# Where the operands of a fused attention, MoE and MLP kernel are split and rounded: VectorE, GpSimd, and which stage

## The chip, the cores and the metric

One Trainium2 chip, one of its cores. The metric is the device time of one execution in microseconds (us). The kernel before takes 1073.9 us, the median of three runs (1072.25 to 1073.95).

## The reference

Three layers, one after the other, in fp32. The outputs of each are the tokens of the next.

```python
# retention-like attention: batch 4, 8 heads, 768 steps, head size 64
state = gamma * state + k[t] (x) v[t];   y[t] = scale * q[t] @ state
# 3072 tokens of 512 -> mixture of 8 experts with a capacity of 384 tokens each:
# all (token, expert) logits in descending order, each token goes to the first expert with room
h = maximum(x[mask] @ w1[e], 0);  out[mask] = h @ w2[e]        # 512 -> 1024 -> 512
# one MLP shared by all tokens
h = x @ w_in;  g = where(h > 0, h, exp(minimum(h, 0)) - 1)     # 512 -> 2048
return g @ w_out                                               # 2048 -> 512
```

`w_in` and `w_out` come as 64-bit words, two per pair of columns, since the kernel rounds them itself ("chunks" below).

## The kernel before, in words

**Three stages.** Attention runs over 48 steps of 64 tokens (4 batches of 12). Then the routing of the first expert (phase 0) is searched with nothing else to do for TensorE. Then eight experts follow one another. Each handles its 384 tokens through both of its own matrices (entries `L1` and `L2` of an order list, 8 each) and then through the shared MLP (entries `F1` and `F2`, 16 each), and scatters its rows to the output. While expert n runs, VectorE searches the routing of later experts, and GpSimd gathers their weights and rows by indirect DMA.

**Products in three parts.** Every matmul operand is split in a high part `hi` (a ScalarE copy to the 32-bit replicated format) and a low part `lo = x - hi` (one subtraction). A product is hi*hi + hi*lo + lo*hi (`mm3`, lines 673 to 676). For the expert matrices `prep` makes `hi` on ScalarE (line 663) and `lo` on GpSimd (line 666), except for the tiles that the table `BYV` gives to VectorE: `L1` number 2 and `L2` number 0 of each expert. For the shared matrices `Wide.parts` makes `hi` (line 274) and `lo` on GpSimd in four pieces of 128 columns (line 279), once per tile. The low part is stored in DRAM and read back for later experts (lines 280 and 270). `which` is 0 for `w_in` and 1 for `w_out`.

**Chunks.** The 32 tiles of `w_in` and `w_out` are loaded as raw words by ScalarE's DMA queue into three staging buffers, and each tile ("chunk") takes three steps: two VectorE instructions (lines 253 and 254), one ScalarE instruction (line 256) and then the load of a later chunk, one GpSimd addition (line 260). During attention `side(j)` is called about twice per step of 64 tokens and starts a step of a chunk on three of eight calls. Ten chunks are done there. In phase 0 of routing the tiles of these ten are split (`early`, before line 806). The other 22 chunks are done during expert 0, at times that `CONV` lists.

**ELU.** For each `F1` tile: Exp on ScalarE from PSUM (line 733), on VectorE min and add, then the max with PSUM, then `gh` on ScalarE (line 740) and `gl = g - gh` on VectorE.

**Order.** The order of instructions on each engine is written out by the program. A model clock advances with the matmuls (`tick`), and `at(us, fn)` puts `fn` in the program when the clock reaches its time. Each engine runs its own queue in that order and waits for what an instruction needs. Router steps are generators; after `yield "v"` the next step is put behind the time `V.free` when the model thinks VectorE is free. `Paced` adds each router, ELU and split instruction to `V.free`. The chunk instructions use `nc.vector` itself, so `V.free` does not count them. VectorE instructions that go through `Paced` have line 215 in the profile.

Of the kernel before, what the change touches and what calls it, by code (L numbers as in the profile page):

```python
# [10 lines left out]
F32 = mybir.dt.float32  # L11
# [13 lines left out]
BIG = 6.0e37  # L25
WARM2 = (2, 2, 2, 2, 14)
WARM3 = (4, 4, 6)
GAP = {"w": 1.8, "x": 1.0, "t": 2.5}
ROOM = {"L1": 2, "L2": 3, "F1": 3, "F2": 3}
BYV = (("L1", 2), ("L2", 0))  # L30
RSTART = 6
PACE, AFTER, HOLD = 0.4, 0.5, 7.0
CONV = {"L1": (0.4, 1.3), "L2": (0.4,), "F1": (0.4, 1.3), "F2": (0.4,)}
ELU = (1.6, 2.6)
NWARM = 18
STAGES, EVERY = 3, 8
SUB = 4
MORE, LOWS = 2, 3
EACH = [(30 - 3 * i, 2 if i == 0 else 3) for i in range(11)]
LEVELS = [(27, 5), (22, 5), (17, 5), (12, 5), (7, 5), (2, 5), (0, 2)]  # L40
# [178 lines left out]
class Wide:  # L219
# [25 lines left out]
        next(self.steps, None)  # L245

    def chunks(self):
        V = self.nc.vector
        for i in range(32):
            t = self.stage.pop(i)  # L250
            lo, hi = t[:, 0:1024:2], t[:, 1:1024:2]
            m = self.raw[i % 2][i // 2].bitcast(I32)
            V.tensor_scalar(m, hi, 3, 0x3FFFFFFF, op0=OP.logical_shift_left, op1=OP.bitwise_and)
            V.scalar_tensor_tensor(m, hi, -0x40000000, m, op0=OP.bitwise_and, op1=OP.bitwise_or)
            yield
            self.nc.scalar.activation(lo, lo.bitcast(U32), AF.Copy, scale=2.0 ** -29)
            if i:
                self.load()
            yield
            self.nc.gpsimd.tensor_tensor(m, m, lo, OP.add)  # L260
            self.done = i + 1
            yield

    def parts(self, which, f, pool, later):


        nc, name = self.nc, ("wis", "wos")[which]
        lo = pool.tile([128, 512], F32R, name=name, bufs=LOWS)
        if (which, f) in self.high:
            nc.sync.dma_start(lo.bitcast(F32), self.low[which, f])  # L270
            return self.high[which, f], lo
        hi = self.high[which, f] = self.pools[which].tile([128, 512], F32R, name="w")
        src = self.raw[which][f]
        nc.scalar.activation(hi, src, AF.Copy)

        def low():
            for c in range(0, 512, 128):
                s = slice(c, c + 128)
                nc.gpsimd.tensor_sub(lo[:, s], src[:, s], hi[:, s].bitcast(F32))  # L279
            nc.sync.dma_start(self.low[which, f], lo.bitcast(F32))  # L280

        later(low)
        return hi, lo


class Router:
# [126 lines left out]
    def search_each(self, ph, Lm, M):  # L413


        nc, w, V = self.nc, self.w, self.V
        vm, vt = w("vm", [128, NCOL, E]), w("vt", [128, 192])
        V.tensor_scalar(vm, M, BIG, -BIG, op0=OP.mult, op1=OP.add)
        V.tensor_tensor(vm, vm, Lm, OP.add)
        yield "v"  # L420
        p = self.pm()
        nc.tensor.transpose(p[:, 0:128], vm[:, 0:16].rearrange("p c e -> p (c e)"), self.ident)
        nc.tensor.transpose(p[0:64, 128:256], vm[:, 16:24].rearrange("p c e -> p (c e)"), self.ident)
        yield "p"
        nc.scalar.activation(vt[:, 0:128], p[:, 0:128], AF.Copy)
        nc.scalar.activation(vt[0:64, 128:192], p[0:64, 128:192], AF.Copy)
        nc.scalar.activation(vt[64:128, 128:192], p[0:64, 192:256], AF.Copy)
        Tb, ni, n = w("Tb", [128, 1], I32), w("ni", [128, 1], I32), w("n", [128, 1])
        cand, pre = w("candf", [128, 8], I32), w("pref", [128, 8], I32)
        cnt, sat = w("cnt", [128, 8], BF), w("satf", [128, 8])  # L430
        scr = [w(f"scr{j}", [128, 192], BF) for j in range(3)]
        yield "a"
        for i, (k, r) in enumerate(EACH):
            J = (1 << r) - 1
            cf = self.jf[:, 0] if i == 0 else cand
            if i > 1:
                V.scalar_tensor_tensor(cand[:, :J], ni.to_broadcast([128, J]), EACH[i - 1][0], pre[:, :J],
                                       op0=OP.logical_shift_left, op1=OP.bitwise_xor)
            for j in range(J):
                V.tensor_scalar(scr[j % 3], vt, cf.bitcast(F32)[:, j:j + 1], 0.0, op0=OP.is_ge, op1=OP.add,  # L440
                                accum_out=cnt[:, j:j + 1])
                if j % SUB == SUB - 1 and j < J - 1:
                    yield "v"
            if i > 1:
                V.scalar_tensor_tensor(Tb, ni, EACH[i - 1][0], Tb, op0=OP.logical_shift_left, op1=OP.bitwise_xor)
            if 0 < i < len(EACH) - 1:
                Jn = (1 << EACH[i + 1][1]) - 1
                V.tensor_tensor(pre[:, :Jn], self.jf[:, i + 1, :Jn], Tb.to_broadcast([128, Jn]), OP.bitwise_xor)
            yield "v"
            p = self.pm()  # L450
            nc.tensor.matmul(p[:, :J], self.same, cnt[:, :J], start=True, stop=True)
            yield "p"
            V.tensor_scalar(sat[:, :J], p[:, :J], self.remp, 0.0, op0=OP.is_ge, op1=OP.add, accum_out=n)
            V.tensor_copy(ni, n)
            if i == 0:
                Jn = (1 << EACH[1][1]) - 1
                self.first_sign(Tb, ni, k)
                V.tensor_tensor(cand[:, :Jn], self.jf[:, 1, :Jn], Tb.to_broadcast([128, Jn]), OP.bitwise_xor)
        V.scalar_tensor_tensor(Tb, ni, 0, Tb, op0=OP.logical_shift_left, op1=OP.bitwise_xor)
        yield "v"  # L460
        p = self.pm()
        nc.tensor.transpose(p[:, :E], Tb.bitcast(F32)[0:E].to_broadcast([E, 128]), self.ident[0:E, 0:E])
        yield "p"
        T = w("T", [128, 1])
        V.tensor_reduce(T, p[:, :E], AX.X, OP.max)
        self.T = T
# [122 lines left out]
def mlps(nc, tc, ctx, a, xd, out, router, wide, ident, acc, rot, pms):  # L589
# [39 lines left out]
    def at(us, fn):  # L629
        heapq.heappush(heap, (clock[0] + us, next(serial), fn))  # L630
# [9 lines left out]
    def run_router():  # L640
        if clock[0] < hold[0]:
            return at(hold[0] - clock[0], run_router)
        after = next(phases[0], None)
        if after is None:
            phases.pop(0)
        if phases:
            at(max(PACE, V.free - clock[0] + PACE) if after == "v" else AFTER, run_router)

    def start_phase(ph):
        phases.append(router.phase(ph))  # L650
# [3 lines left out]
    def prep(ck):  # L654
        kind, n, f = ck
        if kind in ("F1", "F2"):
            WSP[ck] = wide.parts(kind == "F2", f, sb, lambda low: at(0.6, low))
            return
        which = "w1" if kind == "L1" else "w2"
        src = WS[n, which, f // 2][:, (f % 2) * 512:(f % 2) * 512 + 512]  # L660
        hi = sb.tile([128, 512], F32R, name=which + "h", bufs=ROOM[kind])
        lo = sb.tile([128, 512], F32R, name=which + "l", bufs=ROOM[kind])
        nc.scalar.activation(hi, src, AF.Copy)  # L663

        def low():
            (V if (kind, f) in BYV else nc.gpsimd).tensor_sub(lo, src, hi.bitcast(F32))  # L666
            if f in (1, 3):
                gather_w(n, which, f // 2 + 2)

        at(0.6, low)  # L670
        WSP[ck] = (hi, lo)
# [57 lines left out]
    def elu(n, f, p):  # L729
        g = sb.tile([128, CAP], F32, name="g")  # L730
        gh = sb.tile([128, CAP], F32R, name="gh", bufs=4)
        gl = sb.tile([128, CAP], F32R, name="gl", bufs=4)
        nc.scalar.activation(g, p, AF.Exp)  # L733

        def lower():
            V.tensor_scalar(g, g, 1.0, -1.0, op0=OP.min, op1=OP.add)
            V.tensor_tensor(g, p, g, OP.max)

        at(0.5, lower)
        at(ELU[0], lambda: nc.scalar.activation(gh, g, AF.Copy))  # L740
        at(ELU[1], lambda: V.tensor_sub(gl, g, gh.bitcast(F32)))
        GS[n, f] = (gh, gl)

    def do_F2(n, f):
# [57 lines left out]
        return acc.tile([128, 512], F32, name="acc")[:, :384]  # L802

    router.spare = spare
    early = iter(range(wide.done))
    for _ in router.phase(0):
        tick(1.0)
        i = next(early, None)
        if i is not None:
            wide.parts(i % 2, i // 2, sb, lambda low: low())  # L810
        if 0 in router.es and (0, "w1", 0) not in WS:
            gather_w(0, "w1", 0)
            gather_w(0, "w2", 0)
        if 0 in router.idx and (0, 0) not in XG:
            for tb in range(3):
                gather_x(0, tb)
            advance(1)
# [29 lines left out]
    for i, ck in enumerate(seq):  # L847
# [5 lines left out]
            run_todo(n + 1)  # L853
        advance(i + LA)
        if n == 0:
            for us in CONV[kind]:
                at(us, wide.step)
        do[kind](n, f)
    tick(10.0)

# [2 lines left out]
def body(ctx, tc, a, xd, out):  # L863
# [26 lines left out]
        return pms.tile([128, 512], F32, name="pm")  # L890

    router = Router(nc, st, wk, pm, a, L, ident)

    attention(nc, tc, a, xd, ident, side, router.columns)
    acc = ctx.enter_context(tc.tile_pool(name="acc", bufs=4, space=PSUM))
# [93 lines left out]
```

## Time and profile before

| | |
|---|---|
| time, median of 3 runs | 1073.9 us (1072.25 to 1073.95) |
| the profiled execution: its own time, its span | 1078.4 us, 1076.6 us |
| granted TensorE clock, mean | 0.964 |
| busy: TensorE, its weight loads, VectorE, ScalarE, GpSimd | 92%, 83%, 68%, 33%, 39% |
| HBM | 143.75 MB read, 20.97 MB written |

The span runs from the first to the last instruction. The rest of the execution's own time lies around it. A matmul record covers its whole passage through the array, and matmuls follow one another more closely than they last, so the distance of their starts is what counts.

### The profile page before, as it was taken

To read this page: it belongs to the slowest core of one execution; us is meant where nothing else is said; L and a number is where in the kernel's file an instruction comes from. 1 tells how busy PE (TensorE), PEld (TensorE's weight loads), DVE (VectorE), ACT (ScalarE), POOL (GpSimd) and SP (SyncE) were. 2 spreads that over 40 slices of the span, in tenths; PEclk is the share of its full clock that TensorE was granted. 3 is DMA by queue.
4 is the path that set the end of the run, shared out by engine and by line. 5 is a ranking of instruction groups with operands and counts; after the bars stand their busy time and mean duration, and the time that the engine had idled before them with its cause. 6 is when DMAs were issued, how large, how long until landed. Compare 5 with 4: busy or idle time off the path is not lost.

```text
span 1076.6 us, 20354 instructions
## 1 busy us (share of the span) xinstructions
PE 992.8 (92%) x7730; PEld 891.6 (83%) x7730; DVE 732.7 (68%) x2294; ACT 350.5 (33%) x712; POOL 424.3 (39%) x508
## 2 busy tenths in 40 slices
PE   8888938798789999999999999999999999999995
PEld 6777825786678988898899889988998898999994
DVE  4664677879999777977897789778977514331431
ACT  3443422233344323332333233223322333233221
POOL 5465575637898021702170217021702181026001
PEclk9998957899899999999999999999999999999998
DMA  9798535446534263327422742373237326432441
GB/s 367 239 344 289 186 131 189 136 138 194 192 119 161 80 225 120 106 83 228 127 91 89 225 127 89 97 226 118 89 98 226 117 91 212 120 110 84 132 123 49
DMA packets 69635, 166.06 MB, mean 154 GB/s; under 512 B 8992, under 2 KB 15776, under 8 KB 69536
## 3 DMA queue, kind: packets, MB, share of 16 engines
q1 hardware_dynamic: 51152, 101.67, 28.9%
q0 software_dynamic: 13056, 46.14, 13.0%
q10 hardware_dynamic: 5328, 16.94, 4.7%
q8 instruction: 61, 1.00, 0.4%
q14 instruction: 38, 0.31, 0.1%
HBM read 143.75 MB, written 20.97 MB: 153 GB/s over the span
## 4 chain that ended last, share of the span: by engine, by line
PE 71%; DVE 19%; issue 3%; POOL 3%; DMA 2%; ACT 1%; another core or an unknown queue 0%; POOLq 0%; SPq 0%; DVEq 0%; ACTq 0%
PE pr L674 10%; PE pr L676 10%; PE pr L675 10%; PE acc L752 8%; PE acc L753 7%; PE acc L754 7%; DVE scr L215 3%; PE acc L674 3%; PE acc L675 3%; PE acc L676 3%; PE py L138 2%; DVE Tb L215 2%; PE pq L107 2%; DVE g L215 2%; DVE candf L215 2%
## 5 line engine op out<-in xcount | busy, mean ns | idle before, releaser
L674 PE MATMUL pr<-yh,w 128*128 128x384 f32 x512 | 178.0, 348 | 1.3 <-DVE g L215 1.3
L676 PE MATMUL pr<-yh,wis 128*128 128x384 f32 x512 | 174.1, 340 | 0.0
L675 PE MATMUL pr<-yl,w 128*128 128x384 f32 x512 | 172.5, 337 | 0.0
L666 POOL TENSOR_TENSOR w1l<-sw,w1h 128x512 fp32r<-128x512 f32 x56 | 73.0, 1305 | 249.5 <-ACT w1h L663 229.6
L752 PE MATMUL acc<-w,gh 128*128 128x512 f32 x384 | 156.4, 407 | 0.0
L754 PE MATMUL acc<-w,gl 128*128 128x512 f32 x384 | 152.4, 397 | 0.8 <-DVE gl L215 0.8
L753 PE MATMUL acc<-wos,gh 128*128 128x512 f32 x384 | 153.1, 399 | 0.0
L600 POOL DMA_INDIRECT sw<-in_w,es x64 | 66.4, 1038 | 165.0 <-DVE es L215 142.0
L215 DVE TENSOR_SCALAR_CACHE_REDUCE scr<-vt,candf 128x192 bf16<-128x192 f32 x350 | 124.3, 409 | 1.8
L733 ACT ACTIVATE g<-pr 128x384 f32<-128x384 f32 x128 | 62.8, 491 | 183.5 <-PE pr L676 171.8
L740 ACT ACTIVATE gh<-g 128x384 fp32r<-128x384 f32 x128 | 67.1, 525 | 169.5 <-DVE g L215 167.5
L215 DVE TENSOR_SCALAR g<-g 128x384 f32<-128x384 f32 x128 | 52.6, 411 | 84.8 <-ACT g L733 84.0
L674 PEld LDWEIGHTS pr<-yh,w 128*128 128x128 f32 x512 | 97.3, 190 | 7.5 <-DVE g L215 2.0
L675 PEld LDWEIGHTS pr<-yl,w 128*128 128x128 f32 x512 | 97.1, 190 | 4.0
L676 PEld LDWEIGHTS pr<-yh,wis 128*128 128x128 f32 x512 | 96.7, 189 | 0.2 <-POOL wis L279 0.2
L676 PE MATMUL pr<-xh,w1l 128*128 128x384 f32 x256 | 88.4, 345 | 4.1 <-POOL w1l L666 3.9
L215 DVE TENSOR_TENSOR gl<-g,gh 128x384 fp32r<-128x384 f32 x128 | 74.0, 578 | 25.6 <-ACT gh L740 24.4
L674 PE MATMUL pr<-xh,w1h 128*128 128x384 f32 x256 | 89.3, 349 | 1.8 <-ACT w1h L663 1.8
L754 PEld LDWEIGHTS acc<-w,gl 128*128 128x128 f32 x384 | 73.0, 190 | 18.6 <-DVE gl L215 1.2
L674 PE MATMUL acc<-hh,w2h 128*128 128x384 f32 x256 | 87.8, 343 | 0.0
L675 PE MATMUL pr<-xl,w1h 128*128 128x384 f32 x256 | 87.3, 341 | 0.3 <-DVE xl L215 0.3
L676 PE MATMUL acc<-hh,w2l 128*128 128x384 f32 x256 | 85.9, 336 | 0.0
(187 smaller groups left out, 2091.2 us busy)
## 6 DMA issues: line engine op xcount, KB each, us to landing
wis<-low SPq DMA_DIRECT2D x117, 256.0 KB, 3.1
wos<-low SPq DMA_DIRECT2D x117, 256.0 KB, 2.7
Q<-in_kq SPq DMA_DIRECT2D x15, 768.0 KB, 8.0
V<-in_kv SPq DMA_DIRECT2D x15, 768.0 KB, 8.3
stg<-in_w_in ACTq DMA_DIRECT2D x16, 512.0 KB, 4.8
stg<-in_w_out ACTq DMA_DIRECT2D x16, 512.0 KB, 4.2
x_rows<-xs SPq DMA_DIRECT2D x32, 192.0 KB, 7.6
low<-wis SPq DMA_DIRECT2D x16, 256.0 KB, 2.0
```

Source lines behind the costliest of these rows:

```text
L107: nc.tensor.matmul(p[lo, pr, :], q[hi, 1, pr], q[hi, 0, pr], start=True, stop=True)
L215: return getattr(self.eng, name)(*args, **kw)
L600: nc.gpsimd.indirect_dma_start(out=t, out_offset=None, in_=a[f"{which}_{pair}"], in_offset=bass.IndirectOffsetOnAxis(ap=router.es[n][:, :1 ...
L666: (V if (kind, f) in BYV else nc.gpsimd).tensor_sub(lo, src, hi.bitcast(F32))
L674: nc.tensor.matmul(p, ah, bh, start=first, stop=False)
L675: nc.tensor.matmul(p, ah, bl, start=False, stop=False)
L676: nc.tensor.matmul(p, al, bh, start=False, stop=last)
L733: nc.scalar.activation(g, p, AF.Exp)
L740: at(ELU[0], lambda: nc.scalar.activation(gh, g, AF.Copy))
L752: nc.tensor.matmul(p, gh[:, s], wh, start=f == 0, stop=False)
L753: nc.tensor.matmul(p, gh[:, s], wl, start=False, stop=False)
L754: nc.tensor.matmul(p, gl[:, s], wh, start=False, stop=f == 15)
```

## The change

The low parts of the first expert matrix (`L1`) all go to VectorE, those of `L2` all to GpSimd. The low parts of `w_in` go to VectorE, those of `w_out` to GpSimd, in one instruction of 512 columns instead of four of 128. ELU becomes two ScalarE passes (Relu of -h, then Exp of minus that, which is exp(min(h, 0))) and one VectorE step, `max(g - 1, h)`, with later times in the model clock. `side` starts chunk steps on three of every four calls, the split of finished chunks in phase 0 is gone, and chunk instructions go through `Paced`. In expert 0 a chunk step is put in only when the model thinks VectorE free within 1 us, or when the tile is needed within four entries. The pause in the middle of a counting level of the router (`"s"`) is shorter, that after a ScalarE copy (`"a"`) longer.

```diff
-GAP = {"w": 1.8, "x": 1.0, "t": 2.5}
+GAP = {"w": 1.8, "x": 1.0, "t": 1.5}
-BYV = (("L1", 2), ("L2", 0))
-ELU = (1.6, 2.6)
+ELU = (2.0, 2.8, 3.8)
-STAGES, EVERY = 3, 8
-SUB = 4
+STAGES, EVERY = 3, 4
+SUB, AHEAD = 4, 4
     def chunks(self):
-        V = self.nc.vector
+        V = self.V
         def low():
-            for c in range(0, 512, 128):
-                s = slice(c, c + 128)
-                nc.gpsimd.tensor_sub(lo[:, s], src[:, s], hi[:, s].bitcast(F32))
+            (nc.gpsimd if which else self.V).tensor_sub(lo, src, hi.bitcast(F32))
                 if j % SUB == SUB - 1 and j < J - 1:
-                    yield "v"
+                    yield "s"
         if phases:
-            at(max(PACE, V.free - clock[0] + PACE) if after == "v" else AFTER, run_router)
+            wait = V.free - clock[0]
+            at({"v": max(0.0, wait) + PACE, "s": max(0.1, wait - 0.1), "a": 2.0}.get(after, AFTER), run_router)
         def low():
-            (V if (kind, f) in BYV else nc.gpsimd).tensor_sub(lo, src, hi.bitcast(F32))
+            (V if kind == "L1" else nc.gpsimd).tensor_sub(lo, src, hi.bitcast(F32))
-        nc.scalar.activation(g, p, AF.Exp)
-
-        def lower():
-            V.tensor_scalar(g, g, 1.0, -1.0, op0=OP.min, op1=OP.add)
-            V.tensor_tensor(g, p, g, OP.max)
-
-        at(0.5, lower)
-        at(ELU[0], lambda: nc.scalar.activation(gh, g, AF.Copy))
-        at(ELU[1], lambda: V.tensor_sub(gl, g, gh.bitcast(F32)))
+        nc.scalar.activation(g, p, AF.Relu, scale=-1.0)
+        nc.scalar.activation(g, g, AF.Exp, scale=-1.0)
+        at(ELU[0], lambda: V.scalar_tensor_tensor(g, g, -1.0, p, op0=OP.add, op1=OP.max))
+        at(ELU[1], lambda: nc.scalar.activation(gh, g, AF.Copy))
+        at(ELU[2], lambda: V.tensor_sub(gl, g, gh.bitcast(F32)))
-    early = iter(range(wide.done))
     for _ in router.phase(0):
         tick(1.0)
-        i = next(early, None)
-        if i is not None:
-            wide.parts(i % 2, i // 2, sb, lambda low: low())
         if n == 0:
+            late = 2 * (f + AHEAD) if kind in ("F1", "F2") else 0
             for us in CONV[kind]:
-                at(us, wide.step)
+                at(us, lambda: (wide.done < late or V.free < clock[0] + 1.0) and wide.step())
     router = Router(nc, st, wk, pm, a, L, ident)
+    wide.V = router.V
```

## Rows read from the trace of the kernel before

**Rows 1.** Busy time by stage: PE, PEld, DVE, ACT, POOL; clock, DMA share, GB/s.
```profile
0.00:136.00 136.00, 116.80 (x2724) 102.33 (x2726) 77.45 (x195) 53.50 (x124) 72.49 (x110) 0.95 0.80 282
...
176.00:228.00 52.00, 44.47 (x317) 40.66 (x318) 39.34 (x68) 16.78 (x33) 30.44 (x25) 0.90 0.42 141
228.00:320.00 92.00, 76.18 (x415) 65.19 (x414) 85.99 (x195) 37.43 (x75) 68.95 (x102) 0.93 0.53 175
...
427.00:534.00 107.00, 106.00 (x586) 96.13 (x585) 86.37 (x328) 33.90 (x70) 32.85 (x32) 1.00 0.43 134
```

**Rows 2.** Timeline of PE in expert 1: start, duration, line, form.
```profile
400.74 0.34 PE L674 MATMUL pr<-yh,w 128*128 128x384 f32 x1
...
402.84 0.40 PE L752 MATMUL acc<-w,gh 128*128 128x512 f32 x1
...
404.25 0.60 PE L622 MATMUL px<-ident,row 128*128 128x128 f32 x4
```

**Rows 3.** VectorE groups, 176 to 320 us: busy, mean ns, idle before.
```profile
L254 DVE SCALAR_TENSOR_TENSOR w<-stg,w 128x512 int32<-128x512 int32 x22 | 18.2, 829 | 0.8
L253 DVE TENSOR_SCALAR w<-stg 128x512 int32<-128x512 int32 x22 | 18.1, 824 | 0.0
L215 DVE TENSOR_SCALAR g<-g 128x384 f32<-128x384 f32 x15 | 12.1, 805 | 0.5 <-ACT g L733 0.5
L215 DVE TENSOR_TENSOR cmp<-v,cand 128x372 bf16<-128x372 f32 (+1 forms) x12 | 11.6, 1007 | 0.2
...
L215 DVE SCALAR_TENSOR_TENSOR hl<-pr,hh 128x384 fp32r<-128x384 f32 x8 | 4.4, 552 | 1.5 <-ACT hh L688 1.5
```

**Rows 4.** Timeline of VectorE while GpSimd had no tensor work.
```profile
208.43 1.01 DVE L215 TENSOR_TENSOR cmp<-v,cand 128x372 bf16<-128x372 f32 x2
...
209.65 0.42 DVE L253 TENSOR_SCALAR w<-stg 128x512 int32<-128x512 int32 x1
210.10 0.69 DVE L254 SCALAR_TENSOR_TENSOR w<-stg,w 128x512 int32<-128x512 int32 x1
```

**Rows 5.** VectorE's removed ELU pass, 427 to 534 us.
```profile
L215 DVE TENSOR_SCALAR g<-g 128x384 f32<-128x384 f32 x16 | 5.7, 357 | 4.6 <-ACT g L733 4.4
```

**Rows 6.** Timeline in expert 0, 189 to 195 us: VectorE, GpSimd, PE.
```profile
189.09 5.10 DVE L215 TENSOR_TENSOR cmp<-v,cand 128x372 bf16<-128x372 f32 x2
...
192.51 1.27 POOL L666 TENSOR_TENSOR w2l<-sw,w2h 128x512 fp32r<-128x512 f32 x1
...
194.25 0.48 PE L399 MATMUL pm<-cmp,M 128*8 128x31 bf16 x12 [3.03 <-DVE cmp L215]
```

**Rows 7.** Groups of the whole span: busy, mean ns, idle before.
```profile
L215 DVE TENSOR_SCALAR_CACHE_REDUCE scr<-vt,candf 128x192 bf16<-128x192 f32 x350 | 124.3, 409 | 1.8
...
L666 POOL TENSOR_TENSOR w1l<-sw,w1h 128x512 fp32r<-128x512 f32 x56 | 73.0, 1305 | 249.5 <-ACT w1h L663 229.6 <-DVE hl L215 11.5 <-DVE sat L215 5.0
...
L740 ACT ACTIVATE gh<-g 128x384 fp32r<-128x384 f32 x128 | 67.1, 525 | 169.5 <-DVE g L215 167.5 <-issue 2.0
...
L279 POOL TENSOR_TENSOR wos<-w 128x128 fp32r<-128x128 f32 x64 | 33.0, 546 | 5.1 <-ACT w L274 3.0 <-issue 2.0
...
L215 DVE TENSOR_TENSOR w1l<-sw,w1h 128x512 fp32r<-128x512 f32 x8 | 5.5, 686 | 3.6 <-ACT w1h L663 3.6
```

**Rows 8.** Waits of SyncE's DMA queue in attention: total us, times, longest.
```profile
SPq L71 <- DMA stg<-in_w_out: 19.6, 3, 7.8
```

**Rows 9.** Chain that ended last, 25 to 60 us: shares by line.
```profile
by line: DMA V<-in_kv 47.3%; issue 11.9%; PE py L138 8.8%; PE pq L107 8.2%; PE pS L128 7.4%; PE pT L156 4.5%; POOL V L115 4.2%; PE pL L171 3.6%; PE pS L127 3.2%; PE pq L108 1.2%; SPq L71 0.2%; POOLq L115 0.1%
```

**Rows 10.** Timeline of routing phase 0, one of five equal levels.
```profile
144.23 1.45 DVE L215 TENSOR_TENSOR cmp<-v,cand 128x372 bf16<-128x372 f32 x2
```

**Rows 11.** Timeline of GpSimd and ScalarE at the start of expert 0.
```profile
171.54 2.50 POOL L666 TENSOR_TENSOR w1l<-sw,w1h 128x512 fp32r<-128x512 f32 x2
...
182.50 0.63 ACT L663 ACTIVATE w1h<-sw 128x512 fp32r<-128x512 f32 x1 [3.55 <-DMA sw<-in_w,es]
```

**Rows 12.** Waits of PE, 345 to 1060 us: total, times, longest.
```profile
PE pr L676 <- POOL w1l L666: 3.4, 6, 0.7
```

## The prediction

> **What bounds the kernel now.** I read the stages first, then inside each the engine that is waited for. In the table by stage [rows 1] an expert in steady state, 427 to 534 us, has TensorE busy for 106.00 of 107 us at full clock, so little is left there. The timeline of one such expert [rows 2] gives the need: an `F1` tile takes 402.84 - 400.74 = 2.10 us for its 12 matmuls, and six of 512 columns take 1.41 us, 0.235 each. Eight `L1`, eight `L2` and sixteen `F1` tiles at 2.10 us and 144 matmuls at 0.235 us make 101 us; the rest to 107 is transposes, router products and about one us of waiting.
>
> Expert 0 is another matter. Its matmuls run from 176 to 320 us, which is 144 us for the work of 107, and the clock is at 0.90 and 0.93. VectorE is busy for 39.34 + 85.99 = 125.3 us of it [rows 1]. That busy time isn't all work. The groups of this stretch [rows 3] beside the same forms elsewhere [rows 4, 5] show: the chunk's first instruction takes 0.824 against 0.42, its second 0.829 against 0.69, the ELU pass 0.805 against 0.357, a comparison of the router 1.007 against half of 1.01. Over 22, 22, 15 and 12 instructions that is 8.9 + 3.1 + 6.7 + 6.0 = 24.7 us in which VectorE stood inside an instruction. The timeline shows on what [rows 6]: a pair of comparisons begun at 189.09 ends at 194.2, just after the last of an unbroken row of GpSimd tensor instructions (192.51 + 1.27 = 193.8), and TensorE, whose next product needs the comparison, stands 3.03 us. The step `hl`, which has one operand in PSUM and one in SBUF, isn't stretched: 0.552 in this crowded stretch [rows 3]. [...]
>
> **The change, part by part.**
>
> *Attention.* The condition on `sides` is met at 8 to 10, 12 to 14, up to 92 to 94 of 95 calls: 22 chunks, where 10 were done (the title's 24 is not what I count). Twelve more chunks cost VectorE 12 x (0.42 + 0.69) = 13.3 us and GpSimd about 12 x 1.3 = 16 us, in idle time of 136 - 77.45 = 58.5 and 63.5 us [rows 1, 4, 7]. The loads are the doubtful part: 12 x 0.524 = 6.3 MB. The DMA share is 0.80 at 282 GB/s, 352 GB/s when busy; 6.3 MB take 17.9 us, and 0.20 x 136 = 27 us are idle. So the lower bound is 0. For the upper bound: SyncE's loads of keys and values already wait for landings of chunks, 19.6 us in three waits for one of the matrices [rows 8], and in the stretch where this happens 47.3% of 35 us, 16.6 us, of the chain that ended last is a late load of `V` [rows 9]. With 12 more loads beside 10 that grows by 12/10 x 16.6 = 20 us. I take +9, the middle, since the last third of the extra loads falls behind the last load of keys and values.
>
> *Phase 0.* The ten early splits leave. A pair of comparisons beside them took 1.45 us [rows 10] against 1.01 [rows 4], 0.44 on each of five levels, 2.2 us on the only chain that TensorE has there; the small instructions of each level are stretched as well, unknown, bounded by as much again. -2 to -5, I take -3.5.
>
> *Start of expert 0.* Two low parts of 2.50 us stand on GpSimd ahead of the gather of the second weights, and ScalarE then waits 3.55 us for that landing [rows 11]. They move to VectorE (2 x 0.686 [rows 7], ahead of router steps that nobody awaits). I take -2, bounds 0 and -2.5.
>
> *Expert 0.* VectorE: 125.3 - 24.7 = 100.6 us without the stretching. Twelve chunks leave, -13.3; the ELU pass leaves, 16 x 0.357 = -5.7; the new single step costs what `hl` costs, 0.552, against 0.558 for the old max, so nothing; sixteen `w_in` parts arrive, 16 x 0.686 = +11.0; six more `L1` parts, +4.1. That makes 96.7 us. GpSimd: 99.4 us of busy time [rows 1] lose 12 chunks (16), 11 `w_in` tiles at 4 x 0.546 (24), seven `L1` parts (9.1), gain one `L2` part, while sixteen `w_out` tiles at 1.3 cost what eleven at 4 x 0.546 cost less 3: about 49 us, half. With half of GpSimd's work I halve the stretching, 12.3 us: VectorE 109 us. That is about TensorE's own 107. If VectorE keeps the 18.7 us that it is idle now (144 - 125.3), expert 0 takes 128 us, -16; if TensorE sets it alone, 108, -36. I take 120, -24: VectorE's order is now planned with the chunks counted, so router products are placed when their inputs are done, but `w_in` and `w_out` parts are still cut at the same moments by the two engines. ScalarE's added ELU pass (16 x 0.525 [rows 7]) and ten more `hi` copies, less twelve chunk steps, fit in its idle 90 us [rows 1].
>
> *Experts 1 to 7.* The wait for the `L1` low part on GpSimd goes: -3.4 us [rows 12], up to -6 with the weight loads that start late behind it. Against it stands the ELU chain at the first `F1` tiles. There tile 2 needs tile 0's PSUM, one tile (2.10 us) later; two ScalarE passes (taken as the 0.525 of `gh` [rows 7] each) and the step (0.552) take 1.6, which fits by half a us if VectorE is free. `gh` of tile 0 now stands behind the two passes of tile 1, which cannot start before 2.10, so it ends at 2.10 + 3 x 0.525 = 3.7 and `gl` at about 4.2 us, and `F2` wants it at 2 x 2.10 + 2 x 0.235 = 4.67. Four counting steps of the router, each up to 0.409 [rows 7], in front of it would cost 1.2 us, at most 8 us in seven experts. I take +1: together -3, bounds -6 and +5. `L1` parts on VectorE add 6 x 0.686 = 4.1 us an expert and the removed pass takes 5.7: VectorE stays below TensorE. `GAP` and the router's pauses change only the order of work with slack: 0.
>
> Sum: +9 - 3.5 - 2 - 24 - 3 = -23.5. The profiled execution takes 1078.4 us, 4.5 above the median, so 1054.9 for it and 1050 for the median.
>
> **The rivals.**
>
> *Attention eats more* (0.15). The loads cost the full 20 us: -12.5, 1061. For it: the late `V` load [rows 9]. Against: an idle DMA share of 0.20.
>
> *The relief is complete* (0.17). The loads hide (0 to +2) and TensorE alone sets expert 0 (-36): about -42, 1032. For it: 96.7 us of VectorE work below 107. Against: stretching doesn't vanish.
>
> *Slower: chunk loads pace attention* (0.11). VectorE runs in order, and a chunk's first instruction now stands seven `side` calls behind its load instead of fifteen. Two steps of 64 tokens last 136/24 = 5.7 us, so seven calls are about 10 us; a queue wait of up to 7.8 [rows 8] and the transfer could exceed that, and then VectorE, and with it attention, stands once for each chunk. Over 22 chunks it decides from 33/22 = 1.5 us a chunk, where it eats the 32.5 of the other terms; at 3 us a chunk the time is 1073.9 + 66 - 32.5 = 1107, at 2 us 1085.
>
> *The moved parts are held* (0.05). A subtraction with two SBUF inputs may wait for a GpSimd instruction of 1.3 us each time. In expert 0 that is 22 moved parts x 1.3 = 29 us of VectorE, 126 us instead of 97, as busy as before; then expert 0 gains only about 8 and the time is 1066. Against: the eight such parts in the trace average 0.686 with no sign of it [rows 7]. [...]
>
> **How the numbers follow.** The forecast has 0.52, its own range 1038 to 1061. Below 1030 and above 1074 I leave about 0.09 each: 1030 to 1074 reaches to the complete relief and the costlier attention and holds the held parts. Slower by more than 0.2% (what a measurement of this kernel can tell from none) is 0.11 for the slower rival and 0.01 from the edges, within 0.2% 0.05 from the upper edges of the cases that gain and the lower edge of the one that loses, faster the remaining 0.83.
>
> **What would show it.** Attention longer than 136 us, with more waits of SyncE's queue for chunks; phase 0 shorter by some 3 us with comparisons at 1.0 a pair; expert 0 at about 120 us with VectorE busy near 109 and its clock nearer 1; the ELU pass absent and the new step at 0.55; no wait of TensorE for `w1l` on GpSimd. The prediction is wrong if attention grows by more than 20 us, if the comparisons and chunk steps of expert 0 stay stretched, or if waits for `gl` appear at each expert's first `F2`.

## The result, and the profile after

The changed kernel takes 1055.9 us in the median (1055.65 to 1058.36, four runs), the kernel before beside it 1073.1 (1071.2 to 1073.95, four runs): a ratio of 0.985 with the interval 0.983 to 0.987. The profiled execution took 1058.4 us, 20.0 less than the one before.

The table by stage answers to [rows 1]: stretch, its length, busy time of TensorE, its weight loads, VectorE, ScalarE and GpSimd, granted clock, DMA share, GB/s.

```profile
0.00:140.00 140.00, 117.83 (x2722) 103.67 (x2722) 94.26 (x219) 60.38 (x135) 91.32 (x122) 0.94 0.90 319
...
176.00:220.00 44.00, 41.22 (x318) 38.18 (x316) 37.66 (x70) 16.77 (x33) 20.82 (x16) 0.96 0.41 135
220.00:315.00 95.00, 83.20 (x471) 72.17 (x470) 78.96 (x199) 49.78 (x100) 39.02 (x31) 0.96 0.42 147
...
421.00:528.00 107.00, 105.81 (x585) 96.04 (x585) 79.61 (x320) 42.30 (x85) 25.23 (x27) 1.00 0.41 134
```

Attention has taken in VectorE and GpSimd work, expert 0 is shorter and its granted clock is at 0.96 throughout instead of 0.90 and 0.93, and an expert in steady state has gained nothing: TensorE was its bound and still is.

The sum is checked by milestones: starts of matmuls in the timelines, in us from the span's start. The end of attention is that of its last logits product.

| | end of attention | first `L1` | first `L2` of expert 0 | first `L2` of expert 1 | end of last matmul |
|---|---|---|---|---|---|
| before | 136.6 | 175.5 | 187.5 | 332.2 | 1063.6 |
| after | 140.7 | 176.1 | 184.2 | 315.1 | 1043.4 |
| stretch, after less before | +4.1 | -3.5 | -3.9 | -13.8 | -3.1 |

The stretches sum to -20.2, the whole difference of the two profiled executions. Expert 0 is where the time came from. Two rows, from its first `L2` to that of expert 1, before and after, show in what:

```profile
187.50:332.20 144.70, 121.93 (x727) 107.33 (x726) 130.30 (x295) 55.62 (x110) 102.33 (x136) 0.93 0.48 158
```

```profile
184.20:315.10 130.90, 116.58 (x725) 103.42 (x724) 109.59 (x257) 62.80 (x125) 57.19 (x45) 0.96 0.40 139
```

TensorE stands idle for 14.3 us instead of 22.8 (length less busy time), which is 8.5 of the 13.8. Most of the rest is clock: if the share that the granted clock lacks is counted as lost time, that is 0.07 x 144.7 = 10.1 us before and 0.04 x 130.9 = 5.2 after (an estimate from the two rows). The VectorE groups of expert 0, 176 to 303 us, answer to [rows 3] (count, busy us, mean ns, idle before):

```profile
L214 DVE TENSOR_TENSOR wis<-w 128x512 fp32r<-128x512 f32 x16 | 12.8, 798 | 11.2 <-ACT w L273 10.2 <-issue 1.0
L214 DVE SCALAR_TENSOR_TENSOR w<-stg,w 128x512 int32<-128x512 int32 x10 | 8.9, 890 | 0.3
L214 DVE SCALAR_TENSOR_TENSOR g<-g,pr 128x384 f32<-128x384 f32 x15 | 8.2, 544 | 0.0
L214 DVE TENSOR_SCALAR w<-stg 128x512 int32<-128x512 int32 x10 | 7.8, 775 | 0.0
...
L214 DVE TENSOR_TENSOR cmp<-v,cand 128x372 bf16<-128x372 f32 (+1 forms) x12 | 7.4, 662 | 0.2
L214 DVE TENSOR_TENSOR w1l<-sw,w1h 128x512 fp32r<-128x512 f32 x7 | 5.4, 775 | 0.1
```

Ten chunks are left here, the mean comparison is down from 1007 to 662 ns, the ELU pass is gone. What is new is in the first line: VectorE stands 10.2 us for the high parts of `w_in`, which ScalarE makes. TensorE's longest waits in expert 0 (176 to 315 us; total, times, longest):

```profile
PE pr L672 <- DVE g L214: 5.2, 1, 5.2
PE pm L563 <- DVE ohp L214: 2.6, 2, 1.6
PE pm L402 <- DVE sat L214: 2.1, 1, 2.1
```

The one of 5.2 us, at the third `F1` tile, has two delays in front of it, a wait for ScalarE and a hold by GpSimd, as the timeline shows (start, duration, engine; in brackets the idle time before and who ended it):

```profile
224.12 0.81 DVE L214 TENSOR_TENSOR wis<-w 128x512 fp32r<-128x512 f32 x1 [0.91 <-ACT w L273]
...
226.02 1.29 POOL L259 TENSOR_TENSOR w<-w,stg 128x512 int32<-128x512 int32 x1
226.16 3.08 DVE L214 TENSOR_TENSOR cmp<-v,cand 128x372 bf16<-128x372 f32 x2
227.25 1.58 POOL L276 TENSOR_TENSOR wos<-w 128x512 fp32r<-128x512 f32 x1
229.42 0.55 DVE L214 SCALAR_TENSOR_TENSOR g<-g,pr 128x384 f32<-128x384 f32 x1
230.11 0.66 PE L672 MATMUL pr<-yh,w 128*128 128x384 f32 x1 [5.22 <-DVE g L214]
```

A `w_in` part waits 0.91 us on ScalarE, then a pair of router comparisons is held for 3.08 us, until GpSimd's two instructions are over (227.25 + 1.58 = 228.8), and the ELU step that would free PSUM stands behind both. Where the program puts that step counts as well: with earlier ELU times (`i_elu` below) this wait is gone. This wait also cost clock. While TensorE stood, the granted clock fell from 1.00 to 0.50, and it stayed there up to 236.2 us; matmuls of 384 columns then started 0.32 us apart, against 0.17 ahead of the wait:

```profile
229.40:236.20 6.80, 6.09 (x39) 5.34 (x39) 1.87 (x5) 2.36 (x5) 0.00 (x0) 0.50 0.10 39
```

### The profile page after: what moved, and what is told of

Read it like the earlier page. It is cut to its first block, busy times and chain, and to the rows that moved or that the text cites. A ratio compares the mean times of both kernels' runs of the same rounds, so it can differ in the third digit from the quotient of the medians.

```text
span 1056.5 us, 20194 instructions
## 1 busy us (share of the span) xinstructions
PE 985.8 (93%) x7730; PEld 887.7 (84%) x7730; DVE 694.9 (66%) x2230; ACT 416.7 (39%) x840; POOL 326.8 (31%) x348
## 4 chain that ended last, share of the span: by engine, by line
PE 69%; DVE 14%; issue 10%; DMA 3%; ACT 2%; POOL 1%; SPq 0%; ACTq 0%; POOLq 0%; DVEq 0%
PE pr L672 10%; PE pr L674 9%; PE pr L673 9%; PE acc L746 6%; PE acc L747 6%; PE acc L748 6%; PE acc L672 3%; PE acc L674 3%; PE acc L673 3%; DVE scr L214 3%; PE py L137 3%; PE pq L106 2%; DVE w1l L214 2%; PE pS L127 2%; DMA V<-in_kv 1%
## 5 line engine op out<-in xcount | busy, mean ns | idle before, releaser
L214 DVE SCALAR_TENSOR_TENSOR g<-g,pr 128x384 f32<-128x384 f32 x128 | 70.3, 549 | 71.3 <-ACT g L732 71.3
L664 POOL TENSOR_TENSOR w2l<-sw,w2h 128x512 fp32r<-128x512 f32 x64 | 84.0, 1318 | 76.5 <-ACT w2h L661 75.4
L214 DVE TENSOR_TENSOR gl<-g,gh 128x384 fp32r<-128x384 f32 x128 | 71.4, 558 | 44.8 <-ACT gh L734 44.4
L686 ACT ACTIVATE hh<-pr 128x384 fp32r<-128x384 f32 x64 | 31.4, 491 | 144.2 <-PE pr L674 141.6
```

The lines of the kernel that those rows point to most:

```text
L214: return getattr(self.eng, name)(*args, **kw)
L664: (V if kind == "L1" else nc.gpsimd).tensor_sub(lo, src, hi.bitcast(F32))
```

## The experiments

All were timed in five rounds beside the kernel before on the same chip; brackets after a ratio to before are 95% intervals. The changed kernel itself stands at 0.985 [0.983, 0.987]. "Spacing" is the time between the first `L2` matmuls of two experts, from the profiled execution.

**Chunks back to expert 0** (`u_chunks`).

```diff
-STAGES, EVERY = 3, 4
+STAGES, EVERY = 3, 8
-        V = self.V
+        V = self.nc.vector
-                at(us, lambda: (wide.done < late or V.free < clock[0] + 1.0) and wide.step())
+                at(us, wide.step)
```

> The changed kernel with the part on chunks undone: ten chunks in attention, 22 in expert 0 at fixed times, VectorE's chunk instructions not counted in the model clock. Theory (the gain is work taken off VectorE and GpSimd in expert 0): attention ends near 136.6 us again (4 us earlier), expert 0 takes 10 to 15 us longer, the time is 1062 to 1067. Rival (what attention pays is as much as expert 0 gains): within 3 us of 1056.

1069.9 us, 0.996 [0.994, 0.997], somewhat more than the theory had. Attention ends at 137.5, 3.1 earlier than after; expert 0 takes 145.2 us, 14.3 more, and expert 1 takes 109.9, 4 more. The chunk part, these three edits together, is worth 0.011, some 12 us, and most of it lies in expert 0.

**Chunks not counted in the plan** (`u_plan`): `V = self.nc.vector` in `chunks`, nothing else.

> The changed kernel, except that VectorE's chunk instructions are again not counted in the model clock. Theory (work taken away is the gain): within 2 us of 1056, since only ten chunks are left in expert 0. Rival (the order planned with the chunks counted is the gain): 1062 or more, with TensorE's waits for router products in expert 0 as long as before, some 20 us.

1062.9 us, 0.990 [0.987, 0.992]. Expert 0 takes 132.1 and expert 1 109.9 us against 130.9 and 105.9. The time is the rival's, but not its sign: TensorE's waits in expert 0 grow only from 14.3 to 14.8 us, not to some 20. Counting the chunks is worth about 0.005, or 5 us, with intervals that only touch, and most of it shows in expert 1: there TensorE waits 2.0 us for the ELU step and 1.1 for counting steps, against 0.3 in all.

**More chunks in attention** (`i_every3`): `EVERY = 3`, 30 chunks instead of 22.

> The changed kernel with chunk steps on every call in attention: 30 chunks there, 2 in expert 0. Theory (a chunk costs less in attention than in expert 0): attention 3 to 6 us longer than 139, expert 0 6 to 9 us shorter: 1051 to 1056. Rival (loads pace attention from here on): attention above 150 us, 1060 or more.

1061.0 us, 0.989 [0.986, 0.992], whose interval just touches that of the changed kernel. The row of attention:

```profile
0.00:140.00 140.00, 121.16 (x2722) 105.27 (x2722) 111.49 (x235) 66.16 (x143) 106.92 (x130) 0.96 0.96 349
```

Attention ends at 140.8 us with a DMA share of 0.96, so eight more chunks made it no longer. The theory fell: expert 0 gains 3.1 us (127.8) instead of 6 to 9, expert 1 takes 2.4 more (108.3). The routing takes 37.1 us instead of 35.4, but so it does in `i_mix`, `i_elu`, `p_double` and `u_wis`, whose chunks in attention are those of the changed kernel; those 1.7 us can't be put down to the chunks.

**`w_in` parts back to GpSimd** (`u_wis`), still one instruction of 512 columns: `nc.gpsimd.tensor_sub(lo, src, hi...)` for both matrices.

> The changed kernel with the low parts of w_in on GpSimd, in one instruction of 512 columns each. Theory (GpSimd holds VectorE): 16 x 1.3 us more of GpSimd work in expert 0 stretch VectorE's instructions there, expert 0 is 3 to 8 us longer: 1058 to 1063. Rival (VectorE's 11 us less, and its waits of 10 us for the high part on ScalarE, weigh more): 1048 to 1054.

1065.3 us, 0.992 [0.989, 0.995], a little above the theory's range. Expert 0 takes 137.0 us, 6.1 more, though VectorE has sixteen instructions fewer. The groups of VectorE, 176 to 303 us:

```profile
L214 DVE SCALAR_TENSOR_TENSOR w<-stg,w 128x512 int32<-128x512 int32 x10 | 10.9, 1088 | 0.3
...
L214 DVE TENSOR_SCALAR w<-stg 128x512 int32<-128x512 int32 x10 | 9.2, 918 | 0.0
```

The same ten chunks now take 1088 and 918 ns a step instead of 890 and 775: with more work on GpSimd VectorE's instructions are longer. With sixteen parts fewer it is busy for longer in expert 0, 112.8 us against 109.6.

**The old ELU** (`u_elu`): Exp on ScalarE, two VectorE steps, `ELU = (1.6, 2.6)`, as before the change.

> The changed kernel with the old ELU (one ScalarE pass, two VectorE steps, early times). Theory (less VectorE work counts): expert 0 gets 5.7 us of VectorE work more, all of it open to waits on GpSimd, but loses the wait of 5.2 us at the third F1 tile; net +2 to +5, 1058 to 1061. Rival (the later step costs what the shorter one saves): 1051 to 1056. In experts 1 to 7 both expect less than 1 us each.

1057.6 us, 0.984 [0.982, 0.986], no different from the changed kernel. That is two effects that cancel, neither as expected: expert 0 is 5.6 us shorter (125.3), where the theory had it longer, and each of the steady experts is about 0.9 longer (107.4 against 106.5). There TensorE waits for an instruction that VectorE does late, 421 to 850 us:

```profile
PE pr L673 <- DVE xl L214: 5.5, 4, 2.1
PE pm L448 <- DVE scr L214: 3.0, 4, 0.8
```

**Earlier ELU times** (`i_elu`): `ELU = (1.1, 2.0, 3.0)`.

> The changed kernel with the ELU times 1.1, 2.0 and 3.0 instead of 2.0, 2.8 and 3.8. Theory (the step of the first tile stands too late in VectorE's queue, behind a w_in part and a router step): the wait of 5.2 us at the third F1 tile of expert 0 goes, steady experts are unchanged or a few tenths shorter: 1048 to 1053. Rival (VectorE is simply late there): the wait moves to the next tile, 1055 to 1058.

1065.3 us, 0.991 [0.988, 0.994]. My theory fell. The wait of 5.2 us is gone and expert 0 takes 127.5 us, 3.4 less, but experts 2 to 5 take 107.6 to 109.5. There VectorE, in order, stands longer for the inputs of ELU steps (7.6 us instead of 2.7 in expert 3), and the router's counting steps come late (9.9 us of TensorE's waits from expert 1 on, 3.6 in the changed kernel). In expert 0 (172 to 308 us) VectorE still waits for high parts of `w_in`, as long as ever:

```profile
L214 DVE TENSOR_TENSOR wis<-w 128x512 fp32r<-128x512 f32 x16 | 13.4, 835 | 10.4 <-ACT w L273 10.4
```

**Old ELU in expert 0 alone** (`i_mix`), the new form in experts 1 to 7.

```diff
+        if n == 0:
+            nc.scalar.activation(g, p, AF.Exp)
+            ...
+            at(0.5, lower)
+            at(1.6, lambda: nc.scalar.activation(gh, g, AF.Copy))
+            at(2.6, lambda: V.tensor_sub(gl, g, gh.bitcast(F32)))
+        else:
+            ...
```

> The changed kernel with the old ELU in expert 0 alone. From the undone ELU (expert 0 at 125.4 us between first L2 tiles instead of 130.9, steady experts 107.4 instead of 106.5) theory: both gains together, 1050 to 1053. Rival (what expert 0 gains is paid in the next one): 1055 to 1058.

1052.6 us, 0.980 [0.977, 0.982]: faster than both kernels, by 0.005 than the changed one, with intervals that just don't overlap. Expert 0 takes 124.5 us, 6.4 less. Its `w_in` parts and its stretch:

```profile
L214 DVE TENSOR_TENSOR wis<-w 128x512 fp32r<-128x512 f32 x16 | 11.4, 715 | 0.0
```

```profile
180.40:304.90 124.50, 115.98 (x723) 103.33 (x723) 113.06 (x245) 54.87 (x109) 61.44 (x47) 0.96 0.43 147
```

Beside the row of the changed kernel above, VectorE is busy for 3.5 us more (113.1 against 109.6) in 6.4 us less, so its idle time falls from 21.3 to 11.4 us; the 10.2 us of waiting for ScalarE are gone. TensorE's idle time falls from 14.3 to 8.5 us at the same clock, which is nearly all of the 6.4. How much of that is due to the ScalarE pass and how much to the old, earlier times, which came back with it, isn't settled by this run: `i_elu`, with both passes, earlier times and the whole wait for ScalarE, already had 3.4, which leaves some 3 us for the pass. In `u_plan`, whose order differs elsewhere too, the wait for high parts was only 4.8 us and expert 0 no shorter. So most of the 10.2 us seems not to have delayed TensorE.

The profiled execution as a whole is 6.3 us shorter than that of the changed kernel: besides the 6.4 of expert 0, attention, which the edit doesn't touch, ended 7.1 earlier, routing and the start of expert 0 took 3.3 more, and what follows expert 0 took 3.9 more. The 3 us between the medians are therefore not shown to be expert 0's.

**`L1` parts back to GpSimd** (`u_l1`): the table `BYV` of before in the changed kernel.

> The changed kernel with the low parts of L1 on GpSimd again, except the two tiles of the old table. Theory: 3 us more before the first L2 tile, some 4 us more in expert 0, 2.3 us more in each of the last two experts: 1063 to 1066. Rival (the moved subtractions are held as long as they free): within 2 us of 1056.

1080.5 us, 1.007 [1.004, 1.009]: slower than before, and far from both expectations. Expert 0 takes 129.9 us, no longer than in the changed kernel; steady experts take 108.7 to 113.3. Waits of TensorE over four of them, 421 to 850 us, of this kernel, then of the changed one:

```profile
PE pm L449 <- DVE scr L215: 11.1, 4, 4.7
PE pr L673 <- DVE g L215: 3.1, 3, 2.0
PE pr L675 <- POOL w1l L665: 1.6, 4, 0.5
```

```profile
PE pm L448 <- DVE scr L214: 3.6, 4, 0.9
PE pr L672 <- DVE g L214: 1.1, 4, 0.3
```

The wait for the low part on GpSimd, for which the part seemed to be made [rows 12], is 1.6 us; the loss is in the router's counting steps and the ELU step, which VectorE does too late, and in the clock, as the rows of four experts (first `L2` of expert 2 to that of expert 6) show, again of this kernel and then of the changed one:

```profile
422.40:864.80 442.40, 426.11 (x2345) 386.50 (x2344) 318.94 (x1168) 167.76 (x333) 129.32 (x125) 0.99 0.41 129
```

```profile
421.00:847.30 426.30, 421.55 (x2346) 382.66 (x2346) 310.05 (x1205) 167.58 (x333) 99.44 (x101) 1.00 0.42 134
```

Of the 16.1 us TensorE's idle time is 11.5 (16.3 against 4.8); the granted clock of 0.99 instead of 1.00 is worth about 0.01 x 442 = 4.4 us, an estimate.

**The same with the old pauses of the router** (`u_l1_pace`): `yield "v"` and its formula back as well.

> The changed kernel with the low parts of L1 on GpSimd again and also the router's old pauses. Theory (with the short pause the model clock plans VectorE without room, and what GpSimd holds up then lands on TensorE): most of the 24 us that the L1 part alone lost comes back, steady experts at 106.4 us or so, 1060 to 1066. Rival (the loss is the GpSimd work itself, whatever the pauses): 1075 to 1082, as with the L1 part alone.

1099.9 us, 1.023 [1.019, 1.027], with spacings up to 116.6 us, 12.9 us of waits for counting steps and 9.6 for the ELU step. My theory that the shorter pauses cost this time fell: with the longer ones it is more.

**More GpSimd work in experts 1 to 6** (`p_double`). Behind each `L2` low part GpSimd subtracts 448 columns more, into a tile that nothing reads; 48 such instructions.

```diff
+            if kind == "L2" and 0 < n < 7:
+                nc.gpsimd.tensor_sub(junk, src[:, :448], hi[:, :448].bitcast(F32))
```

> The changed kernel with one added GpSimd subtraction of 448 columns into an unused tile behind each L2 low part of experts 1 to 6 (48 in all; no one reads them). Theory (GpSimd holds VectorE instructions with two SBUF operands): in experts 1 to 6 the group w1l on VectorE grows from 0.85 us to above 1.1, the groups with a PSUM operand (hl, the ELU step) stay at 0.55, and TensorE waits more for the router's counts: 1062 to 1075. Rival (the stretching has another cause, such as the order or ScalarE): all groups as they were and 1056.

1088.3 us, 1.011 [1.008, 1.014], though nobody waits for the added work. VectorE's groups over four experts, 421 to 850 us, first of the changed kernel, then of this one:

```profile
L214 DVE TENSOR_TENSOR w1l<-sw,w1h 128x512 fp32r<-128x512 f32 x33 | 29.5, 895 | 7.8 <-ACT w1h L661 7.8
L214 DVE SCALAR_TENSOR_TENSOR hl<-pr,hh 128x384 fp32r<-128x384 f32 x33 | 18.3, 555 | 13.7 <-ACT hh L686 13.7
L214 DVE SCALAR_TENSOR_TENSOR Tb<-ni,Tb 128x1 int32<-128x1 int32 x38 | 13.4, 353 | 0.1
```

```profile
L214 DVE TENSOR_TENSOR w1l<-sw,w1h 128x512 fp32r<-128x512 f32 x30 | 34.5, 1150 | 3.0 <-ACT w1h L662 3.0
...
L214 DVE SCALAR_TENSOR_TENSOR Tb<-ni,Tb 128x1 int32<-128x1 int32 x39 | 26.9, 690 | 0.1
L214 DVE SCALAR_TENSOR_TENSOR hl<-pr,hh 128x384 fp32r<-128x384 f32 x32 | 17.7, 554 | 6.1 <-ACT hh L689 6.1
```

The low part takes 1150 instead of 895 ns, a step of one single column 690 instead of 353, and `hl`, which reads PSUM, 554 as ever. Steady experts take 5 to 6 us more, and the time is above the theory's range. Waits of TensorE for counting steps are 16.7 us in four places (340 to 1080 us), against 3.6 in the changed kernel; none of its waits there is for GpSimd, so the added work didn't cost time by delaying GpSimd's own. The mean granted clock of experts 2 to 5 is 0.97 instead of 1.00: in expert 3, for one, TensorE stood 4.17 us up to 554.4, and the clock was at 0.50 from 552.7 to 559.5. This shows the hold as a cause of time, apart from all else in the change; the waits that it made cost a second time, in clock.

**Before, without the early splits** (`b_noearly`): `pass` in place of `wide.parts` in phase 0.

> The kernel before without the splits in phase 0 of routing; the ten tiles are then split in expert 0, on GpSimd in four pieces each. Theory: phase 0 is 3.5 us shorter (35.4 instead of 38.9 us from the end of attention to the first L1 matmul), expert 0 longer by 5 to 12 us for 22 us more of GpSimd work: 1076 to 1083. Rival (GpSimd has room in expert 0): 1070 to 1071.

1075.2 us, 1.001 [0.999, 1.003]. Routing is shorter by the same 3.5 us as in the changed kernel (35.4), and expert 0 4.9 us longer (149.6): a loan, paid back. The time and expert 0 are just below the theory's ranges.

**Before, with the `L1` parts on VectorE and the new pauses and gap** (`b_l1_pace`).

> The kernel before with the low parts of L1 on VectorE and those of L2 on GpSimd, the router's new pauses and the shorter gap of the row transposes; chunks, ELU, w_in parts and phase 0 as before. Theory (L1's parts off GpSimd shorten the stretches in which VectorE is held): 2.3 us less in each of the last two experts, 4 us less before the first L2 tile, 4 to 8 us less in expert 0: 1058 to 1066. Rival (the L1 part is worth something only together with the new ELU and the chunks): 1070 or more.

1072.7 us, 0.999 [0.997, 1.001], no gain that can be told from none. The rival's time holds: in this order these parts together are worth next to nothing.

## Why the prediction was right, and where it was off

The forecast was 1050 us with a range of 1038 to 1061; the median is 1055.9. The sum of -23.5 stands against -20.2 in the profile, and part of that closeness is luck: attention cost 4.9 us less than forecast, the start of expert 0 gave 1.9 more, and together they hide two thirds of the 10.2 us by which expert 0 fell short.

**Attention, +9; measured +4.1.** The cost was put on the wrong wait. The sum let the late load of `V` grow with the chunks; in the stretch of [rows 9] it fell to 23.9% of the chain from 47.3%, though 22 chunks were done. SyncE's queue did wait longer for chunk landings, 53.9 us in all instead of 43.7, mostly off the chain. The 4 us themselves aren't firm: the nine kernels with 22 chunks ended attention between 133.6 and 141.4 us (138.2 in the mean), the four with ten between 136.6 and 137.5 (137.1). The rival by which chunk loads pace attention is refuted: VectorE's first chunk steps waited for landings 2.2 us in all, 0.1 a chunk, where it needed 1.5.

```profile
L214 DVE TENSOR_SCALAR w<-stg 128x512 int32<-128x512 int32 x22 | 12.4, 562 | 2.2 <-DMA stg<-in_w_in 2.2
```

**Phase 0, -3.5; measured -3.5.** Five pairs of comparisons kept VectorE busy for 5.0 us, 1.00 a pair against 1.45 [rows 10], as forecast, and the small steps of a level are unheld as well. But the step counted a stage where it should have counted the work: `b_noearly` shows that the splits are owed in expert 0, 4.9 us there. The debt is in the forecast, since the sum of expert 0 has all sixteen tiles of each matrix, but as a gain this term stands by itself only on paper.

```profile
L214 DVE TENSOR_TENSOR cmp<-v,cand 128x372 bf16<-128x372 f32 x10 | 5.0, 543 | 0.2
```

**Start of expert 0, -2; measured -3.9.** Right in direction, more than the bound of 2.5.

**Expert 0, -24; measured -13.8.** This is the term that was mis-sized, and by its last step. The sum's 144 us run from the first `L1` of expert 0 to that of expert 1, 175.5 to 319.5 before; in the changed kernel it is 127.1 us, 176.1 to 303.2 (-16.9; the -13.8 is between first `L2` matmuls). The start of expert 0, counted beside it, lies in this stretch too, so the forecast for it was -26. There VectorE is busy for 105.5 us, where I had 109. What failed is the choice between 128 and 108: I let part of VectorE's idle time go because its order was planned better. It didn't go: it is 21.6 us, before 18.7. The 128 us for "VectorE keeps its idle time" was right.

Of the idle time, 10.2 us is the wait for ScalarE's high parts of `w_in`. I had written that ScalarE's added work would "fit in its idle 90 us". Its total fits; its place in the queue doesn't, because high parts stand behind two ELU passes and a `gh` that waits for VectorE, and VectorE then waits for the high parts. `i_mix` takes the added pass out of expert 0 alone, the wait vanishes and 6.4 us come back there; judging by `i_elu`, about half of that is due to the ELU times instead. What else keeps VectorE's idle time where it is stays open.

Halving the stretching was about right for the groups that the sum named. Against the unheld durations (543 ns in phase 0, [rows 4, 7]) the rows of after give 12 x 0.119 for comparisons, 10 x (0.355 + 0.200) for chunks, 16 x 0.112 and 7 x 0.089 for the moved parts, 9.4 us in all, where I had 12.3. (I had taken half of a pair's 1.01 us for a comparison; alone it takes 543 ns, since the two of a pair overlap: 10 x 0.543 = 5.4 us in 5.0 us of busy time.) But the list was short. The router's one-column step, in the stretch of [rows 3], isn't in it:

```profile
L215 DVE SCALAR_TENSOR_TENSOR Tb<-ni,Tb 128x1 int32<-128x1 int32 x7 | 6.4, 911 | 0.0
```

At 154 ns unheld (last section) that is 5.3 us more before, counted as work, and the router's small steps are still held after (five `pre` steps at 975 ns in the mean, 176 to 303 us, against 180 to 190 in phase 0). Nor did the sum name what the time was made of, TensorE's waits and its clock.

**Experts 1 to 7, -3; measured -3.1.** The size came out by luck. The wait for `w1l` on GpSimd is gone from the trace as said. Yet the gain lies elsewhere: spacings are 105.9 to 106.8 us as before (106.3 to 106.4) while the router works, since waits for counting steps (3.6 us) and for the ELU step (1.4) have taken its place, and only the last two experts are shorter, by 2.3 and 1.1 us. The price of the ELU chain was right for steady experts (those 1.4 us), not for expert 0, where the step came late and gave the 5.2 us; I had priced it over seven experts and left the first out.

**Router pauses and gap, 0.** No test isolates them in the changed kernel. That order costs nothing in general was wrong: earlier ELU times (`i_elu`), uncounted chunks and the old pauses beside the old table moved the time by 0.5 to 1.6%.

**The moved parts are held** was half right. In steady experts the `L1` part takes 895 ns instead of 686 [rows 7]; 33 x 0.209 is 6.9 us in four experts, off the path. `p_double` shows the same with more GpSimd work: 1150 ns.

**What the parts are worth isn't additive.** Taken out of the changed kernel, the table of `L1` parts is worth 0.022, some 24 us; put into the kernel before, with the new pauses, 0.001. In `u_l1` the four spacings from expert 2 to expert 6 are together 16 us longer than in the changed kernel; the waits shown above account for 11 of them (15.8 against 4.7), all but 1.6 of them waits for VectorE, and the clock for most of the rest. The one-column step there takes 729 ns as against 353, so VectorE is held as in `p_double`. Before it took 705 as well (443 to 870 us) and TensorE waited little for counting steps, 2.6 us from 345 us on. So the hold alone isn't the cause. My reading is that the order with the new ELU and its later steps has no room for it, but that is not shown: no run has the old `L1` table together with the old ELU in the changed kernel, and none the `L1` part alone in the kernel before.

## What to carry to other kernels

Where VectorE and GpSimd work side by side, count GpSimd's tensor instructions as time of VectorE too: in `p_double` 48 instructions that nobody waits for cost some 30 us, about 0.6 each, nearly what VectorE would take for such a part itself (0.69). When a pass moves to an engine with idle time, don't ask whether the sum fits, but what is queued behind it and who waits for that. An engine's wait is worth what it delays on the path: of VectorE's 10.2 us of waiting only some 3 could be traced to the time. Count a wait of TensorE twice where the granted clock falls with it, as at the wait of 5.2 us, behind which it was 0.50 up to 236.2 us. A gain in one stage that only leaves work for the next one is to be charged there, and a part should be timed both taken out of the new kernel and put into the old one.

## What the runs showed of the hardware

A small instruction was held about as long as a large one. Where the subtraction of 512 columns went from 686 ns to 895 in the changed kernel (421 to 850 us) and 1150 in `p_double`, the step on one single column (two operands in SBUF) took 353 and 690 ns on average, and 154 in phase 0 of the changed kernel, where GpSimd had no tensor work:

```profile
L214 DVE SCALAR_TENSOR_TENSOR Tb<-ni,Tb 128x1 int32<-128x1 int32 x6 | 0.9, 154 | 0.0
```

An instruction with one 32-bit operand in SBUF and a 32-bit result, the chunk's first, was held as well (420 ns unheld [rows 4], 775 in expert 0 of the changed kernel, 918 in `u_wis`). The counting step, 32 bits in and bf16 out, took 408 to 409 ns in the mean in steady experts of both kernels, `u_l1`, `u_l1_pace`, `p_double`, `b_l1_pace` and `i_mix`, and steps of 384 columns with one operand in PSUM took 0.54 to 0.56 us. What sets the two kinds apart is not shown. Two held steps ended with a row of GpSimd instructions, or soon after: in the changed kernel a pair of comparisons, 1.01 us unheld, took 3.08 and ended at 226.16 + 3.08 = 229.24, 0.4 us after the last of GpSimd's two (228.8), and in the kernel before the one-column step took 4.26 us, until 205.64, behind three GpSimd instructions of which the last ended at 204.36 + 1.27 = 205.63.

```profile
201.38 4.26 DVE L215 SCALAR_TENSOR_TENSOR Tb<-ni,Tb 128x1 int32<-128x1 int32 x1
...
204.36 1.27 POOL L666 TENSOR_TENSOR w2l<-sw,w2h 128x512 fp32r<-128x512 f32 x1
```
